# Second transform step as eight 64x32 matmul tiles side by side, its inverse as eight 32x64 tiles, complex products over all 128 partitions

## The chip, the cores and the metric

One Trainium2 chip (trn2), one core. The metric is the device time of one execution in microseconds, the median of several runs; lower is better.

Words used below: TensorE leaves its results in PSUM (the tiles `ps` and `pst` of the traces); an evacuation is the copy from there by ScalarE or VectorE (1.02 us for one of 128x1024 on ScalarE), after which the buffer is free again. A gemm is one of branch B's large matrix products. A burst is a row of branch A's matmuls between two pieces of gemm. A drain is the time that TensorE loses on entering and leaving a burst (0.22 us, measured in experiment 2). The granted clock is the share of TensorE's full clock that it was allowed in a stretch of the profile (1.0 or 0.5 in the profiled runs before and after).

## The reference

A forward and backward pass of two branches that share a layer norm. Branch A is a long convolution per channel by FFT (2048 points, 1024 channels) behind a four-tap shift filter; branch B is a gated MLP (1024 to 3584 and back). Cut to what matters:

```python
def _A_ref(q, k, v, shift_k, ssm_k, ssm_D):
    # kv = (k filtered by 4 taps) * v
    kv_f = rfft(pad(kv, 2S));  kf_f = rfft(pad(ssm_k, 2S))
    y = irfft(kv_f * kf_f)[:S] + kv * ssm_D
    return q * y
def _B_ref(x, W_gate, W_up, W_down):
    gate = x @ W_gate; up = x @ W_up
    return ((gate * (gate > 0)) * up) @ W_down
xn = layernorm(A_q)
out = A_q + _A_ref(xn, ...) + _B_ref(xn, ...)
# returned: out and the gradients of all nine inputs for grad_out
```

Per channel group of 128 (eight groups) the kernel needs three forward transforms (filter h, gradient g, product kv) and three inverse ones (gradient of kv, y, gradient of h). Each transform is two steps of small matmuls, with a transpose between them.

## The kernel before

TensorE runs the gemms of branch B all the time. The steps of branch A are a generator whose matmuls are put between the gemms', a few at each `yield`; `ns` is how much gemm time is to pass. Matmuls and loads get the current priority, ScalarE's and VectorE's work of the branch a late one, and a scheduler then orders every engine's queue at build time.

```python
def mm(self, out, lhsT, rhs, start=True, stop=True):
    self.pri.now();  self.nc.tensor.matmul(out, lhsT=lhsT, rhs=rhs, start=start, stop=stop)
def act(self, out, in_):           # nearly every evacuation of the branch's PSUM tiles: ScalarE (the transposes of h: VectorE, vcopy)
    self.pri.late(); self.nc.scalar.copy(out=out, in_=in_)
# self.ps: 2 PSUM buffers of 4 KB per partition for the whole branch; the gemms have 4 of 2 KB

def h_tile(self, st):              # filter: 32 transposes of 64 columns a group
    ...
    for r in range(16):
        for u in range(2):
            self.nc.tensor.transpose(pst[64*u:64*u+64, r, :], hv[:, r, u, :], self.identA[:])
    self.vcopy(hT[:, 0:16, :], pst[:])

def fwd2(self, Bf, F, ns):         # second step: 32 matmuls, 128x128 by 128 columns
    for k0 in range(0, NB1, 8):
        ps = self.ps.tile([P, 8, P], F32, name="ps2", tag="aps")
        for j in range(8):
            self.mm(ps[:, j, :], self.FW[:, k0 + j].rearrange("p a k -> p (a k)"), Bf[:, k0 + j, :])
        kh, kl = k0 // 16, k0 % 16
        rows = slice(64 * kh, 64 * kh + 64)
        self.act(F[rows, 0, kl:kl + 8, :], ps[0:64])      # real rows
        self.act(F[rows, 1, kl:kl + 8, :], ps[64:128])    # imaginary rows
        yield ns

def cmul(self, X, Z, conj, name):  # per half: products in full width, sums in 4 half-width ones
        ...
        self.tt(t1[:], X[:, :, ks, :], Z[:, :, ks, :], ALU.mult)
        self.tt(t2[:, 0], X[:, 0, ks, :], Z[:, 1, ks, :], ALU.mult)
        self.tt(t2[:, 1], X[:, 1, ks, :], Z[:, 0, ks, :], ALU.mult)
        for kh in range(2):
            rows = slice(64 * kh, 64 * kh + 64); kk = ...
            self.tt(Q[0:64, kk, :], t1[rows, 0], t1[rows, 1], ALU.add if conj else ALU.subtract)
            self.tt(Q[64:128, kk, :], t2[rows, 0], t2[rows, 1], ALU.subtract if conj else ALU.add)

def inv_a(self, Q, ns):            # inverse of the second step: 32 matmuls, 128x128 by 128 columns
    for k0 in range(0, NB1, 8):
        ps = self.ps.tile([P, 8, P], F32, name="ps3", tag="aps")
        for j in range(8):
            self.mm(ps[:, j, :], self.IA[:, k0 + j]..., Q[:, k0 + j, :])
        self.act(C[:, :, k0:k0 + 8, :], ps[:].rearrange("p k (cp i) -> p cp k i", i=2))
        ...
        yield ns
```

## Time and profile before

| | before |
|---|---|
| median of all runs of the first comparison | 1979.49 us (1974.76 to 1981.42) |
| TensorE busy in the profiled run | 1926.1 of 1974.6 us |
| VectorE, ScalarE busy | 988.9 us, 717.0 us |
| second step and its inverse: matmuls | 2 x 768, full array |
| first start to first start of the next gemm, 8 of these | 0.446 us |

How to read it: a matmul's duration in the profile is its latency (219 ns in the second step, where the next one starts after 0.056 us). What it costs TensorE's stream is the distance from its start to the next one's, so bursts are read from the start of the first matmul to the start of the gemm's next one. The lines themselves stand in the prediction.

### The profile page before, as it was taken

How to read it: one execution, taken by the hardware profiler on the slowest of the kernel's cores; microseconds unless marked ns; L12 is line 12 of the kernel's file. 1: busy time of each engine (PE TensorE's matmuls, PEld its weight loads, DVE VectorE, ACT ScalarE, POOL GpSimd, SP SyncE). 2: the span in 40 equal slices, each digit the busy share in tenths (PEclk: the TensorE clock that was granted, in tenths of full speed). 3: DMA queues.
4: the chain of work that ended last, by engine and by line, in shares of the span. 5: the costliest groups of instructions: out<-in, count | busy, mean ns of one | idle time of the engine just before them, and what ended most of it. 6: DMA issues, size and time to landing. Idle time of an engine off the chain costs nothing.

```text
span 1974.6 us, 27321 instructions
## 1 busy us (share of the span) xinstructions
PE 1926.1 (98%) x11022; PEld 916.2 (46%) x11022; DVE 988.9 (50%) x1457; ACT 717.0 (36%) x945; POOL 15.5 (1%) x36
## 2 busy tenths in 40 slices
PE   6899999999999999999999999999999999999998
PEld 3345445445444444444444445544444444444443
DVE  5879669578677756556356437300122122222222
ACT  5675365456446428347346455411000000000000
POOL 1000000000000000000000000000000000000000
PEclk9999999999999999999999999999999999999999
DMA  9954666974675674372753442593999854455451
GB/s 264 254 156 134 173 184 162 213 196 128 168 189 127 196 205 139 97 197 75 216 162 118 115 144 75 150 302 133 205 232 256 173 134 119 120 125 124 122 125 40
DMA packets 615168, 318.32 MB, mean 161 GB/s; under 512 B 450169, under 2 KB 584321, under 8 KB 615041
## 3 DMA queue, kind: packets, MB, share of 16 engines
q1 hardware_dynamic: 604544, 295.60, 58.7%
q10 hardware_dynamic: 9216, 16.78, 2.9%
q0 software_dynamic: 1280, 4.20, 0.6%
q8 instruction: 86, 1.41, 0.3%
q14 instruction: 42, 0.34, 0.1%
HBM read 141.36 MB, written 95.44 MB: 120 GB/s over the span
## 4 chain that ended last, share of the span: by engine, by line
PE 71%; DVE 4%; issue 2%; ACT 2%; DMA 1%; SPq 0%; DVEq 0%; ACTq 0%
PE ps_w L733 19%; PE ps_x L850 19%; PE ps_o L816 10%; PE ps_d L733 9%; PE ps L65 5%; PE ps_g L602 3%; PE ps_u L602 3%; PE ps_h L602 3%; ACT H L69 1%; DVE flp L291 1%; DVE t L73 1%; DVE ru L681 1%; PE pst L280 0%; DVE Y L73 0%; DVE ru L665 0%
## 5 line engine op out<-in xcount | busy, mean ns | idle before, releaser
L733 PE MATMUL ps_w<-ugs,xn_nat 128*128 128x512 bf16 x1792 | 402.6, 379 | 1.6 <-DMA xn_nat<-xn_d 1.6
L602 PEld LDWEIGHTS <-xnT 128*128 128x128 bf16 x1792 | 170.9, 98 | 212.0 <-issue 19.1
L733 PEld LDWEIGHTS <-xn_nat 128*128 128x128 bf16 x1792 | 170.2, 98 | 200.8 <-issue 7.2
L863 ACT ACTIVATE w<-xn,m 128x512 f32<-128x512 bf16 x32 | 24.3, 806 | 559.5 <-issue 317.2
L602 PE MATMUL ps_g<-wg,xnT 128*128 128x512 bf16 x896 | 210.4, 383 | 10.8 <-DVE ru L665 4.1
L602 PE MATMUL ps_h<-wdT,goT 128*128 128x512 bf16 x896 | 208.9, 381 | 3.0 <-DMA wdT<-in_B_W_down_dram 3.0
L733 PE MATMUL ps_d<-g_nat,hs 128*128 128x512 bf16 x896 | 204.8, 379 | 4.1 <-DMA hs<-h_d 4.1
L602 PE MATMUL ps_u<-wu,xnT 128*128 128x512 bf16 x896 | 206.4, 379 | 0.0
L850 PE MATMUL ps_x<-wuT,guT 128*128 128x512 bf16 x896 | 198.6, 379 | 0.0
L850 PE MATMUL ps_x<-wgT,ggT 128*128 128x512 bf16 x896 | 198.6, 379 | 0.0
L816 PE MATMUL ps_o<-wd,hT 128*128 128x512 bf16 x896 | 193.6, 379 | 0.0
L771 ACT CAST wi<-ps_w 128x512 bf16<-128x512 f32 x112 | 65.5, 586 | 207.2 <-PE ps_w L733 191.9
L680 ACT CAST gh<-ps_h 128x512 bf16<-128x512 f32 x112 | 65.4, 585 | 197.6 <-PE ps_h L602 126.0
L850 PEld LDWEIGHTS <-guT 128*128 128x128 bf16 x896 | 87.7, 98 | 105.7
L850 PEld LDWEIGHTS <-ggT 128*128 128x128 bf16 x896 | 87.7, 98 | 105.7
L816 PEld LDWEIGHTS <-hT 128*128 128x128 bf16 x896 | 87.7, 98 | 105.7
L602 PEld LDWEIGHTS <-goT 128*128 128x128 bf16 x896 | 85.2, 98 | 102.7 <-issue 10.1
L291 DVE STREAM_TRANSPOSE flp<-B 128x1024 f32<-128x1024 f32 x48 | 90.4, 1935 | 84.7 <-ACT B L69 84.5
L852 DVE CUSTOM_DVE_ANT_0 gx<-ps_x,gy 128x512 f32<-128x512 f32 x32 | 22.1, 692 | 217.9 <-PE ps_x L850 217.9
L733 PEld LDWEIGHTS <-hs 128*128 128x128 bf16 x896 | 83.8, 98 | 101.4 <-issue 5.9
L69 ACT CAST C<-ps 128x1024 bf16<-128x1024 f32 x96 | 97.3, 1017 | 61.1 <-PE ps L65 61.1
L291 DVE STREAM_TRANSPOSE flp<-C 128x1024 f32<-128x1024 f32 x48 | 89.8, 1928 | 52.6 <-ACT C L69 52.3
(156 smaller groups left out, 1699.7 us busy)
## 6 DMA issues: line engine op xcount, KB each, us to landing
ug_d<-ru SPq DMA_DIRECT2D x112, 256.0 KB, 3.0
ugs<-ug_d SPq DMA_DIRECT2D x112, 256.0 KB, 4.5
wg<-in_B_W_gate_dram SPq DMA_DIRECT2D x56, 256.0 KB, 4.2
wu<-in_B_W_up_dram SPq DMA_DIRECT2D x56, 256.0 KB, 3.9
h_d<-ht SPq DMA_DIRECT2D x112, 128.0 KB, 2.1
hs<-h_d SPq DMA_DIRECT2D x56, 256.0 KB, 4.3
out_dram<-wi SPq DMA_DIRECT2D x56, 256.0 KB, 2.5
gt<-in_grad_out_dram SPq DMA_DIRECT2D x32, 256.0 KB, 3.5
```

The lines of the kernel that those rows point to most:

```text
L65: self.nc.tensor.matmul(out, lhsT=lhsT, rhs=rhs, start=start, stop=stop)
L69: self.nc.scalar.copy(out=out, in_=in_)
L73: self.nc.vector.tensor_tensor(out=out, in0=in0, in1=in1, op=op)
L291: self.nc.vector.transpose(out=df[:, c0:c0 + 32, :], in_=sf[:, c0:c0 + 32, :])
L602: self.nc.tensor.matmul(ps[:], lhsT=xT[:, kt * P:(kt + 1) * P], rhs=w(kt), start=(kt == 0), stop=(kt == self.DT - 1))
L680: nc.scalar.copy(out=gh[:], in_=ps[:])
L733: self.nc.tensor.matmul(ps[:], lhsT=lhsT(st), rhs=rhs(st), start=(st == 0), stop=(st == self.ST - 1))
L771: nc.scalar.copy(out=wo[:, d, :], in_=ps[:])
L816: nc.tensor.matmul(ps[:], lhsT=hT[:, kt, :], rhs=self.wd[:, kt, oc], start=(kt == 0), stop=(kt == self.FT - 1))
L850: nc.tensor.matmul(ps[:], lhsT=T[:, kt, :], rhs=W[:, kt, oc], start=(i == 0), stop=(i == n - 1))
L852: V.tensor_tensor_reduce(out=gx[:, oc], in0=ps[:], in1=gy[:, oc], scale=1.0, scalar=0.0, op0=ALU.add, op1=ALU.add, accum_out=m[:, ob:ob + 1])
L863: nc.scalar.activation(out=w[:, oc], in_=xn[:, oc], func=ACT.Identity, scale=m[:, 5:6], bias=m[:, 4:5])
```

## The change

The intent: use the array for matmuls that fill it only in part by running eight at once, and get the spectra into a layout in which real and imaginary parts lie on the same partitions, so that the evacuation and the complex products work on all 128 partitions. The filter's first step becomes a full-array one for that layout. Core of the diff (tables and index arithmetic cut):

```diff
-        self.FW = con.tile([P, NB1, 2, 64], BF16, name="FW")
-        self.IA = con.tile([P, NB1, 2, 2, NB1], BF16, name="IA")
+        self.FW = con.tile([P, NB1, 2, NB1], BF16, name="FW")
+        self.IA = con.tile([P, 16, 2, 2, NB1], BF16, name="IA")
+        self.RH = con.tile([P, 2, 2, 2, NB1], BF16, name="RH")
 ...
     def h_tile(self, st):
         for r in range(16):
-            for u in range(2):
-                self.nc.tensor.transpose(pst[64 * u:64 * u + 64, r, :], hv[:, r, u, :], self.identA[:])
+            self.nc.tensor.transpose(pst[:, r, :], hv[:, r, :], self.identA[:])
 ...
+    def fwd1_filter(self, hT, sD, ns):          # h: full-array matmuls of 512 columns, 2 per yield
+                self.mm(ps[:, 512 * jj:512 * jj + 512], self.RH[:, r0 // 16]..., hT[:, r:r + 4, :]...)
 ...
     def fwd2(self, Bf, F, ns):
+        for j0 in range(0, 4, 2):
+            for j in range(j0, j0 + 2):
+                ps = self.ps.tile([P, 2, 2, 2, P], F32, name="ps2", tag="aps")
+                for ri in range(2):
+                    for m in range(2):
+                        for q in range(4):
+                            for e in range(2):
+                                rows, l = slice(64 * e, 64 * e + 64), 8 * q + 2 * j + m
+                                self.mm(ps[32 * q:32 * q + 32, e, ri, m, :], self.FW[rows, l, ri, :], Bf[rows, l, :])
+                self.act(F[:, 2 * j:2 * j + 2]..., ps[:]...)          # all 128 partitions
+            yield 2 * ns
 ...
     def cmul(...):
-            for kh in range(2): ... four sums over 64 partitions
+            self.tt(Q[:, g, 0], t1[:, :, 0], t1[:, :, 1], ALU.add if conj else ALU.subtract)
+            self.tt(Q[:, g, 1], t2[:, 0], t2[:, 1], ALU.subtract if conj else ALU.add)
 ...
     def inv_a(self, Q, ns):
+        for j0 in range(0, 4, 2):
+            ps = [self.ps.tile([P, 2, 2, 2, P], F32, name="ps3", tag="aps") for _ in range(2)]
+            for j in range(2):
+                for m in range(2):
+                    for ri in range(2):
+                        for q in range(4):
+                            for e in range(2):
+                                rows, x = slice(32 * q, 32 * q + 32), 8 * e + 2 * (j0 + j) + m
+                                self.mm(ps[q // 2][64 * e:64 * e + 64, q % 2, j, m, :], self.IA[rows, x, ri]...,
+                                        Q[rows, 2 * (j0 + j) + e, ri, P * m:P * m + P], start=ri == 0, stop=ri == 1)
+            for h in range(2):
+                self.act(C[:, :, 2 * h:2 * h + 2, 2 * j0:2 * j0 + 4, :], ps[h][:]...)
+            yield 2 * ns
```

## The prediction

> **What bounds the kernel now.** I read the page first (busy times, slices, the chain), then the groups by shape, the TensorE waits, and three short stretches of the TensorE timeline, because the change lives inside a few bursts of matmuls.
>
> The page (busy line; TensorE and ScalarE in 40 slices; the chain):
> ```profile
> PE 1926.1 (98%) x11022; PEld 916.2 (46%) x11022; DVE 988.9 (50%) x1457; ACT 717.0 (36%) x945; POOL 15.5 (1%) x36
> ...
> PE   6899999999999999999999999999999999999998
> ...
> ACT  5675365456446428347346455411000000000000
> ...
> PE 71%; DVE 4%; issue 2%; ACT 2%; DMA 1%; SPq 0%; DVEq 0%; ACTq 0%
> ```
> See: TensorE is at nine tenths or more in every slice but the first two and the last. The transform branch (slices 3 to 26, where ScalarE is busy) never makes it fall below that. So the time is what TensorE streams, plus small pauses; VectorE and ScalarE work counts only where TensorE waits for it.
>
> TensorE's own waits between 98 and 1290 us, where the branch runs:
> ```profile
> PE ps L65 <- ACT H L69: 5.1, 9, 1.4
> PE ps_g L602 <- DVE ru L665: 4.1, 3, 2.2
> PE ps_d L733 <- DMA hs<-h_d: 4.1, 3, 1.8
> PE ps L65 <- DVE flp L291: 2.0, 2, 1.1
> ```
> See: what ScalarE and VectorE cost TensorE is about 11 us in total (the first, second and fourth lines), so even a large saving there can bring no more than this.
>
> The groups the change touches, by shape:
> ```profile
> L69 ACT CAST H<-ps 64x1024 bf16<-64x1024 f32 x64 | 64.4, 1006 | 6.9 <-PE ps L65 5.7
> L65 PE MATMUL ps<-flp,FW 128*128 128x128 bf16 x768 | 58.5, 219 | 1.3 <-DVE flp L291 1.0 <-ACT H L69 0.4
> ...
> L73 DVE TENSOR_TENSOR GH<-t 64x1024 bf16<-64x1024 bf16 x64 | 43.8, 684 | 0.9
> ...
> L280 PE MATMUL pst<-ident,hn 128*64 128x128 bf16 x256 | 16.0, 278 | 0.0
> L280 PEld LDWEIGHTS <-hn 128*64 128x64 bf16 x256 | 14.9, 204 | 3.0 <-issue 3.0
> ```
> The 219 ns of a matmul is its latency; what it takes from the stream is the distance to the next start. The timeline gives that (start, length, what, count):
> ```profile
> 115.46 1.89 PE L602 MATMUL ps_h<-wdT,goT 128*128 128x512 bf16 x8
> 117.18 0.61 PE L65 MATMUL ps<-flp,FW 128*128 128x128 bf16 x8
> 117.63 1.89 PE L602 MATMUL ps_h<-wdT,goT 128*128 128x512 bf16 x8
> ...
> 195.73 3.62 PE L602 MATMUL ps_u<-wu,xnT 128*128 128x512 bf16 x16
> 199.28 1.05 PE L65 MATMUL ps<-flp,RB 128*64 128x512 bf16 x8
> 200.26 3.63 PE L602 MATMUL ps_h<-wdT,goT 128*128 128x512 bf16 x16
> ...
> 218.12 1.08 PE L65 MATMUL ps<-kp,gks 128*32 128x128 bf16 x64
> 219.13 1.04 PE L602 MATMUL ps_g<-wg,xnT 128*128 128x512 bf16 x4
> ```
> See three things. The eight second-step matmuls take 117.63 - 117.18 = 0.45 us, 0.056 us each, and the eight gemm matmuls before them 1.72 us, 0.216 each: no pause on entering or leaving. The 64 column-tiled matmuls of the tap gradient take 219.13 - 218.12 = 1.01 us, 0.0158 each: four tiles really do run side by side (0.056/4 = 0.014), with some 0.1 us left over. And the burst in two column tiles: from 195.73 to 200.26 is 4.53 us, of which 16 x 0.216 = 3.46 and four side-by-side rounds x 0.216 = 0.86 are stream; 0.21 us remain. A burst in another tile shape therefore costs about 0.2 us to enter and leave.
>
> [...] The transposes of h now have 64 columns and their loads show 204 ns against 98 for a contiguous 128x128; whether a strided load of 128 columns is faster, no row shows. [...]
>
> **The change, part by part.** The second step and its inverse are each called 24 times (8 groups, 3 spectra).
>
> Second step and inverse, TensorE. Before: 2 x 768 full-array matmuls x 0.056 = 86 us, in the gemm's own shape, so no drains. After: 128 small matmuls per call, eight side by side, so 16 rounds instead of 32 matmuls: 2 x 24 x 16 x 0.056 = 43 us if eight tiles run as four do. But each burst now leaves the gemm's shape. The order of the built kernel has 49 bursts for the second step (47 of 64 matmuls, 2 of 32) and 55 for the inverse (46 of 64, the rest fragments): 104 x 0.2 = 21 us. So 86 becomes 64: -22 us. Half the stream is saved and half of that is given back to drains.
>
> First step of the filter: before 64 matmuls 64x512 in pairs, 32 rounds x 0.216 = 6.9, plus 17 bursts x 0.2 = 3.4; after 64 full-array ones x 0.216 = 13.8 without drains: +3.5 us.
>
> Transposes of h: before 256 of 64 columns. The first 32 start at 93.68 and the gemm follows at 95.60, so 1.92 us per group, 8 x 1.92 = 15.4. After: 128 of 128 columns, no drain. At 0.056 each (load hidden) 7.2 us; at 0.11, the pace of the present pairs, 14.1; at 0.22, if a strided column costs what it costs now and nothing is loaded in parallel, 28. I choose 0.09, 11.5 us: -4 us.
>
> ScalarE: 192 copies of 64x1024 at 1006 ns become 96 of 128x1024 at about 1020 (the B and C rows' sort): 193 to 98 us, -95 us. The other copies keep their number. VectorE: the four half-width sums per half product become two in full width; 192 rows of 684 ns become 96 of the 128x1024 form, 685 ns, so 131 to 66 us, -66 us. Neither is on the path, except for the 11 us of waits. I give half of these back: -6 us, with one shortened cold-clock spell after the 2.2 us wait counted in. Table building shrinks by a few us of ScalarE and VectorE work early on, beside TensorE: 0.
>
> Sum: -22 + 3.5 - 4 - 6 = -28.5, which from 1977.6 gives 1949. I put the prediction at 1952, for the rival that follows.
>
> **The rivals.** (a) Eight tiles don't get fed. A burst is 128 instructions in 8 x 0.056 = 0.45 us, 3.5 ns each; in the tap gradient the same 128 take 1.01 us, so nothing in this trace shows such a pace. [...] Within the tap burst pairs start about 4 ns apart[...], which speaks for it. If decoding only holds the tap gradient's pace, 6144 x 0.014 = 86 us plus 21 us of drains stand against 86: +21, and the total is about 1993. In between ([...]0.64 us a burst) the gain of 22 nearly vanishes: about 1970.
> (b) The evacuation paces it. The inverse takes both PSUM buffers of the branch in one burst, and the second step fills both too, so the next burst waits for two ScalarE copies, 2.04 us, plus one or two of the gemm's of 0.59. Between bursts lie about 16 gemm matmuls, 3.46 us. That just fits; where it doesn't, TensorE pauses. At 0.1 us per burst this is +10 us: about 1960.
> (c) The relief is worth more than its waits, since VectorE's complex products stand before the gemm's own VectorE step (the 2.2 us wait on ru). All 11 us and some drains less: about 1940.
> (d) The strided loads of h come out at 0.22 us: +13 in place of -4, about 1968.
>
> **Range and chances.** The full-rate case (six in ten) lies at 1940 to 1958, the partial one (three in ten) at 1958 to 1978, the unfed one (one in ten) above. Low 1937, high 1975. 2% is 39.5 us, so faster needs under 1938: the 29 us plus 11 from elsewhere. Faster 0.11, within 2% 0.85, slower 0.04.
>
> **What would show it.** Right: the second step's 64 small matmuls take about 0.45 us to the next gemm start minus the drain (0.55 us with it), the inverse the same; the gap before them is about 0.1 us over 0.216; TensorE's waits on H and ru fall; TensorE busy stays at 97 to 98%; ScalarE falls to about 620 us and VectorE to about 920. Wrong: bursts of 0.7 us and more[...], waits of the branch's matmuls on ScalarE's C, F or K copies growing, transposes of h at 0.2 us each. The prediction falls if the burst is longer than 0.7 us, or if the time drops by more than 40 us, which would mean that the branch's VectorE and ScalarE work held TensorE in a way its waits don't show.

In rival (a) the 0.64 us a burst was an assumed value, and "decoding" stands for whatever sets the pace of the tap gradient's burst (0.0158 us a matmul measured). The "cold-clock spell" is in the trace: 3.4 us at a granted clock of 0.5 after the wait of 2.24 us that ends at 498.90.

## More of the kernel before

After branch A has ended, `out_phase` begins; ScalarE's queue issues its loads `ya`, `xe`, `xr` into a pool that is laid into the memory which branch A's pools had. The tables `FW` and `IA` took 8 KB per partition each.

## The result, and the profile after

The changed kernel takes 1968.46 us (1965.94 to 1969.93, 4 runs) against 1979.49 before. The ratio is 0.9946, 95% interval 0.9924 to 0.9969. Ratios here are the mean time of one kernel's runs over that of the other's of the same rounds, so not quite the ratio of the medians that are quoted. The step is clear of noise, but it is 11 us where 25 to 28 were foretold.

The page of the changed kernel, the same lines as shown of before:
```profile
PE 1894.5 (96%) x15264; PEld 881.7 (45%) x15502; DVE 912.3 (46%) x1374; ACT 615.8 (31%) x852; POOL 15.3 (1%) x37
...
PE   6899999999999989999999999899999999999998
...
ACT  5654354344444425444344444311000000000000
...
PE 87%; DMA 4%; DVE 4%; issue 3%; ACT 1%; SPq 0%; ACTq 0%; DVEq 0%
```
ScalarE lost 101 us and VectorE 77, about as foretold (to 622 and 923). TensorE stays the bound. Of its matmul records 238 are missing (15264 of 15502; the weight loads are complete), so its busy time and the "0.16 <-issue" remarks below are partly gaps in the record; where the gemm's first matmul after a burst is missing, its weight load dates it.

The groups by shape (columns: busy us, mean ns, idle before):
```profile
L66 PE MATMUL ps<-flp,FW 64*32 64x128 bf16 x3072 | 36.2, 221 | 1.6 <-DVE flp L302 1.0 <-ACT B L70 0.5
...
L70 ACT CAST H<-ps 128x1024 bf16<-128x1024 f32 x32 | 30.9, 1019 | 10.8 <-PE ps L66 10.8
...
L74 DVE TENSOR_TENSOR GH<-t 128x1024 bf16<-128x1024 bf16 x32 | 20.8, 685 | 0.0
...
L291 PEld LDWEIGHTS <-hn 128*128 128x128 bf16 x128 | 9.3, 150 | 1.4
```
A full-width copy or sum takes what a half-width one took (1019 against 1006 ns, 685 against 684), so their number is what counts. The strided load of 128 columns takes 150 ns where the one of 64 took 204 (a contiguous 128x128 takes 98); step and tile shape differ at once between the two, so no run parts them. 16 transposes follow each other at 0.063 us.

The first bursts of the second step on TensorE's timeline:
```profile
117.96 1.89 PE L636 MATMUL ps_h<-wdT,goT 128*128 128x512 bf16 x8
119.78 0.75 PE L66 MATMUL ps<-flp,FW 64*32 64x128 bf16 x64
...
125.75 0.75 PE L66 MATMUL ps<-flp,FW 64*32 64x128 bf16 x64
126.43 0.82 PE L636 MATMUL ps_u<-wu,xnT 128*128 128x512 bf16 x2
```
In the second burst shown no record is missing: 126.43 - 125.75 = 0.68 us from the first small matmul to the gemm. Before it the gap is 119.78 - 117.96 - 8 x 0.216 = 0.09 us. So a burst of 64 costs 0.78 us, not the 0.65 of the prediction's sum (0.45 and 0.2).

The start times of single records show where in the burst it goes. These are read from the same trace (ns from the burst's first start; number of the matmul in the burst):

```
matmul   1   2   8 |   9  16 |  17  24 |  25  32 |  33   34   35   36  ...  63   64
start    0   4  24 |  66  90 | 122 145 | 178 201 | 253  261  270  278  ... 503  537
```

Four rounds of eight come every 56 ns, as hoped: eight tiles do run side by side. Then, after exactly 32 matmuls and 33 weight loads (the 33rd load starts at 181 ns), 65 instructions, there is a pause of 52 ns, and from there on a matmul every 8.3 ns, with its load in between: 4.17 ns per instruction in the mean. Of the 93 whole bursts of both kinds 92 show the break at this place.

A second thing is new at the end of branch A. TensorE and, under it, ScalarE and VectorE in the same stretch:
```profile
1252.79 0.76 PE L66 MATMUL ps<-GH,IA 32*64 32x128 bf16 x64
1253.71 13.11 PE L767 MATMUL ps_w<-ugs,xn_nat 128*128 128x512 bf16 x59 [0.16 <-issue]
1273.38 1.89 PE L66 MATMUL ps<-RB,flp 128*128 128x64 bf16 x32 [6.56 <-DVE flp L302]
```
```profile
1253.56 1.01 ACT L70 CAST C<-ps 128x1024 bf16<-128x1024 f32 x1 [1.80 <-PE ps L66]
1253.69 0.34 ACTq L835 DMA_DIRECT2D ya<-y_d  x1
...
1263.11 0.59 ACT L805 CAST wi<-ps_w 128x512 bf16<-128x512 f32 x1 [7.11 <-DMA xe<-xn_d]
...
1268.65 1.02 ACT L70 CAST C<-ps 128x1024 bf16<-128x1024 f32 x1
```
```profile
1269.69 3.63 DVE L302 STREAM_TRANSPOSE flp<-C 128x1024 f32<-128x1024 f32 x2 [1.94 <-ACT C L70]
```
The last inverse ends on TensorE at 1253.6. One of its two C copies runs at once; the other is in ScalarE's queue behind the loads ya, xe and xr of the next phase, which wait for buffers and for each other (the last is issued at 1267.79), and starts at 1268.65. The flip follows, and TensorE, which has run out of gemms put before this point, waits 6.56 us. Before the change ScalarE's queue held those loads behind the last C copy.

From the start times of all matmuls I take, for each part, the time from the end of the gemm before it (last start and 0.216) to the start of the gemm after it. Sums in us of the two profiled runs:

| part | foretold | before | after | change |
|---|---|---|---|---|
| second step, 95 and 49 bursts | } -22 | 44.8 | 39.1 | -5.8 |
| its inverse, 99 and 55 bursts | } | 45.7 | 40.7 | -5.0 |
| transposes of h | -4 | 16.0 | 8.1 | -7.9 |
| first step of h | +3.5 | 11.2 | 19.0 | +7.8 (4.9 of it two waits on the copy of h) |
| first step of kv | (waits: -6) | 17.0 | 10.1 | -6.9 (its waits on ScalarE gone) |
| last step of h's inverse | 0 | 8.7 | 16.3 | +7.7 (the wait above) |
| pauses inside the gemms | (in the -6) | 23.4 | 25.9 | +2.5 |

They add to -7.6, where the two profiled runs differ by 7.5.

A third thing the sums hide. The first of the two waits on the copy of h ends at 406.06 us, and after it TensorE is granted half its clock for 3.4 us (`--windows`: length, busy time of each engine, granted clock, DMA):
```profile
406.20:409.60 3.40, 3.18 (x8) 1.18 (x8) 1.68 (x5) 1.01 (x1) 0.00 (x0) 0.50 0.46 116
```
The weight loads of the gemm there, which are all on record, come every 0.43 us and not every 0.216, so this wait of 2.8 us cost some 1.7 us more. Between 98 and 1290 us the kernel before has one such stretch (3.4 us at 499, after a wait of 2.24 us), the changed kernel three (3.4 us at 406, 3.4 at 710, 6.8 from 1270 on, the last one beginning within the wait of 6.56 us): 13.6 us for 3.4, which can have cost 5.1 us at most (half of the 10.2 us more).

### The profile page after: what moved, and what is told of

Its sections match the earlier page's. It is cut to its first block, busy times and chain, and to the rows that moved or that the text cites. A ratio compares the mean times of both kernels' runs of the same rounds, so it can differ in the third digit from the quotient of the medians.

```text
span 1967.1 us, 35885 instructions
## 1 busy us (share of the span) xinstructions
PE 1894.5 (96%) x15264; PEld 881.7 (45%) x15502; DVE 912.3 (46%) x1374; ACT 615.8 (31%) x852; POOL 15.3 (1%) x37
## 4 chain that ended last, share of the span: by engine, by line
PE 87%; DMA 4%; DVE 4%; issue 3%; ACT 1%; SPq 0%; ACTq 0%; DVEq 0%
PE ps_w L767 19%; PE ps_x L884 19%; PE ps_o L850 10%; PE ps_d L767 10%; PE ps_h L636 8%; PE ps_u L636 8%; PE ps_g L636 8%; PE ps L66 6%; DMA h_d<-ht 1%; DVE flp L302 1%; DVE ru L699 1%; DMA ln_x<-in_A_q_dram 0%; DVE tap L74 0%; DMA g_nat<-in_grad_out_dram 0%; DMA xe<-xn_d 0%
## 5 line engine op out<-in xcount | busy, mean ns | idle before, releaser
L767 PE MATMUL ps_w<-ugs,xn_nat 128*128 128x512 bf16 x1731 | 391.6, 380 | 8.1 <-issue 4.5
L767 PE MATMUL ps_d<-g_nat,hs 128*128 128x512 bf16 x863 | 197.9, 381 | 8.0 <-DMA g_nat<-in_grad_out_dram 3.9
L636 PE MATMUL ps_u<-wu,xnT 128*128 128x512 bf16 x866 | 201.6, 379 | 2.8 <-issue 1.9
L70 ACT CAST C<-ps 128x1024 bf16<-128x1024 f32 x96 | 92.6, 1016 | 53.0 <-PE ps L66 51.9
```

The lines of the kernel that those rows point to most:

```text
L636: self.nc.tensor.matmul(ps[:], lhsT=xT[:, kt * P:(kt + 1) * P], rhs=w(kt), start=(kt == 0), stop=(kt == self.DT - 1))
L767: self.nc.tensor.matmul(ps[:], lhsT=lhsT(st), rhs=rhs(st), start=(st == 0), stop=(st == self.ST - 1))
```

## The experiments

All were run on a chip beside the kernel before; the ratio is to it. `e1_pad` is an edit of the changed kernel; all later ones are edits of `e1_pad`, except `e10_before_h_early`, which is one of the kernel before. All gave correct results but one.

**1. The buffers back where they lay.** `e1_pad`:
```diff
         self.gs_all = con.tile([P, self.NG, 4], F32, name="gs_all")
+        self.pad = con.tile([P, 3840], BF16, name="pad")
+        V.memset(self.pad[:, 0:2], 0.0)
```

> The changed kernel with one unused 7.5 KB tile added beside the tables, so that the branch's other buffers lie where they lay before the change; no arithmetic differs. Theory (the smaller tables moved the next phase's buffers, its loads were put ahead of the last inverse copy on ScalarE, and TensorE stood 6.6 us for the last flip): that wait goes, the last two bursts of 16 are apart again, and the time is 6 to 8 us under the changed kernel's, about 1961, 0.990 to 0.992 of before. Rival (the wait has another cause, or the loads are only late by chance): the time stays within 2 us of the changed kernel's, 0.994 to 0.995 of before. The small bursts cost 0.78 us each in both.

Measured: 1963.14 us, ratio 0.9920 (0.9907 to 0.9932), so some 5 us under the changed kernel's 0.9946, a little less than expected; the two intervals, of different rounds, still overlap, and the profiled spans differ by 6.7. The same stretch on TensorE and on ScalarE:
```profile
1254.28 0.76 PE L66 MATMUL ps<-GH,IA 32*64 32x128 bf16 x64
...
1263.62 0.63 PE L66 MATMUL ps<-RB,flp 128*128 128x64 bf16 x16
```
```profile
1255.05 1.93 ACT L70 CAST C<-ps 128x1024 bf16<-128x1024 f32 x2 [1.80 <-PE ps L66]
...
1268.25 0.41 ACTq L837 DMA_DIRECT2D ya<-y_d  x1
```
Both C copies run at once, the loads follow 11 us later, and the wait is gone, by nothing but an unused tile. The stall is an effect of where the smaller tables let the next phase's buffers lie.

**2. Bursts of 32.** `e2_bursts32`:
```diff
                 self.act(F[:, 2 * j:2 * j + 2]..., ps[:]...)
-            yield 2 * ns
+                yield ns
 ...  in inv_a, inside the loop over j:
+                if j == 0:
+                    yield ns
 ...
-            yield 2 * ns
+            yield ns
```

> As e1_pad, but each burst of 64 small matmuls is cut into two of 32 with gemm matmuls between (some 96 more bursts). Theory ([...]32 pairs, run at eight tiles side by side, 0.0070 us each; only what comes after them is held to 0.0083 after a pause of 0.05): a burst of 32 takes 4 x 0.056 + 0.19 = 0.41 us, none shows the pause, and the total is 96 x (2 x 0.41 - 0.78) = 4 us above e1_pad, in a range of 2 to 8. Rival (eight tiles are slow throughout[...]): a burst of 32 streams at 0.0090 each, takes 0.48 us, and the total is 96 x 0.19 = 18 us above e1_pad.

Measured: 1974.97 us, ratio 0.9981 (0.9967 to 0.9994): 12 us above `e1_pad`, between the two expectations. The bursts decide it:
```profile
116.96 1.89 PE L640 MATMUL ps_h<-wdT,goT 128*128 128x512 bf16 x8
118.78 0.42 PE L66 MATMUL ps<-flp,FW 64*32 64x128 bf16 x32
119.35 1.67 PE L640 MATMUL ps_h<-wdT,goT 128*128 128x512 bf16 x7 [0.16 <-issue]
```
The gemm's first record is missing; its weight load dates it to 119.13. Over all bursts of 32 the median, with the gap before, is 0.442 us for the second step (0.455 for the inverse), and none of the second step's 92 has the break after its 32nd matmul, for there is none. Four rounds of 0.056 are 0.223, so entering and leaving costs 0.219, a little more than the 0.19 I had put in. The rival, slow tiles throughout, wanted 0.48. Two of 0.442 against one of 0.776 for 46 pairs is +5.0 us, two of 0.455 against 0.786 for 47 pairs +5.8, together 10.8; my 4 had the drains too small. That this is close to the 12 is partly luck. In the sums over all bursts the inverse takes 11.2 us more than in `e1_pad`, since 21 of its bursts stand 0.27 to 0.41 us in their middle (in the one at 193.48 us ScalarE is still copying C until 193.81), and the pauses inside the gemms are 6.0 us less: the wait on g_nat near 700 us, 4.0 us in `e1_pad`, isn't there. The medians leave both out. They also give the price of the break: at the full rate a burst of 64 would take 0.445 + 0.219 = 0.66 and takes 0.78, so 0.11 to 0.12 us, some 11 us over 93 bursts.

**3. What holds the second half.** `e5_n64`, wrong:
```diff
-    self.mm(ps[32 * q:32 * q + 32, e, ri, m, :], self.FW[rows, l, ri, :], Bf[rows, l, :])
+    self.mm(ps[32 * q:32 * q + 32, e, ri, m, 0:64], self.FW[rows, l, ri, :], Bf[rows, l, 0:64])
```

> Wrong results on purpose: as e1_pad, but the second step's small matmuls stream 64 columns instead of 128 (the same values are copied out twice). It measures what holds the second half of a burst to 0.0083 us per pair. If it is the rate at which instructions are handed on (a fixed time per instruction), the second half stays at 0.0083 and a burst still takes at least 0.55 us with its 0.22 of entering and leaving. If it is the eight tiles' streaming or conflicts between them, it falls towards half. [...]

Measured in one look (1959.84 us, results wrong as intended). A burst:
```profile
119.72 0.70 PE L66 MATMUL ps<-flp,FW 64*32 64x64 bf16 x64
120.35 1.90 PE L640 MATMUL ps_h<-wdT,goT 128*128 128x512 bf16 x8
```
120.35 - 119.72 = 0.63 where 128 columns took 0.68. Its start times: the first 32 matmuls begin within 124 ns, in rounds of 29 ns where 128 columns took 56; the next one begins at 227 ns, and from there a matmul every 8.3 ns again. So half the columns halve the rounds of the first half and leave the second's pace alone: that pace is the same time per pair with both widths, 4.17 ns per instruction in the mean. The weight loads, the same in both kernels, can start faster than that: the first 33 of this burst come 3.3 ns apart. The pause is not a fixed time: it is 103 ns here for 52 with 128 columns, and in both kernels the first matmul after it starts 27 to 28 ns after the first small matmul of the burst has ended by its record (226 ns long with 128 columns, 199 with 64; new starts at 253 and 227). By the records 65 instructions have started when the pause begins. What holds the next ones back until then is not shown. The pace falls in with the first branch of my expectation.

**4. The relief given back.** `e3_half_width`:
```diff
-                self.act(F[:, 2 * j:2 * j + 2]..., ps[:]...)
+                for rows in (slice(0, 64), slice(64, 128)):
+                    self.act(F[rows, 2 * j:2 * j + 2]..., ps[rows]...)
 ...
-            self.tt(Q[:, g, 0], t1[:, :, 0], t1[:, :, 1], ...)
-            self.tt(Q[:, g, 1], t2[:, 0], t2[:, 1], ...)
+            for rows in (slice(0, 64), slice(64, 128)):
+                self.tt(Q[rows, g, 0], t1[rows, :, 0], t1[rows, :, 1], ...)
+                self.tt(Q[rows, g, 1], t2[rows, 0], t2[rows, 1], ...)
```

> As e1_pad, but the second step's ScalarE copies and the sums of the complex products are done in two halves of 64 partitions, which gives back the 95 us of ScalarE and the 66 us of VectorE that the change saved; TensorE's instructions are the same. Theory (TensorE sets the time, the relief counts only in its waits): 2 to 9 us above e1_pad. Rival (the relief is what the change earned, the small tiles earn nothing): 15 us or more above e1_pad, that is no better than before.

Measured: 1981.16 us, ratio 1.0015 (1.0000 to 1.0029). The rival was right: 18 us above `e1_pad`, no better than before, with TensorE's bursts still at 0.776. TensorE's waits here (total, times, longest):
```profile
PE ps_g L640 <- DVE ru L703: 5.0, 5, 1.5
...
PE ps L66 <- ACT H L70: 3.7, 7, 1.1
...
PE ps L66 <- ACT C L70: 3.6, 2, 2.9
```
Summed over all bursts, second step, inverse and first step of kv take 5.9 + 4.1 + 4.0 = 14 us more than in `e1_pad`, and the pauses inside the gemms 9 us more, with the 5.0 of the first line; the first step of h takes 2 us less. These waits are not those of before given back; they are larger than them. My theory fell here.

**5. Which half of it.** `e8_act_half` has the first edit of the last experiment alone, `e9_dve_half` the second.

> As e1_pad, with the second step's ScalarE copies alone in two halves (95 us of ScalarE given back). If the 18 us of e3_half_width come from the evacuation, which a burst that fills both PSUM buffers cannot run ahead of: 10 to 15 us above e1_pad, and e9_dve_half within 4 us. If they come from VectorE's complex products standing before the gemm's own VectorE steps: within 4 us of e1_pad here, 10 to 15 above there. If they add: both in between.

> As e1_pad, with the sums of the complex products alone in two halves (66 us of VectorE given back). Numbers as told for e8_act_half: within 4 us of e1_pad if evacuation is the cause of the 18 us, 10 to 15 above it if VectorE's queue is.

Measured: 1975.56 us, ratio 0.9981 (0.9968 to 0.9994), with ScalarE's 95 us given back, and 1970.06 us, ratio 0.9961 (0.9948 to 0.9974), with VectorE's 66. That is 12 and 8 us above `e1_pad`'s 0.9920, and together about the 18 of both. They add, though by the recorded numbers the first alone lies in its branch of 10 to 15; per 10 us of added work each costs TensorE 1.2 to 1.3 us. In `e8_act_half` TensorE's waits show where: ScalarE's copies, mostly. In `e9_dve_half` 4.8 us more are pauses inside the gemms, among them 2.1 us of waits on ru, and 4.1 us lie in the inverse, 3.3 of them in one burst at 334 us.
```profile
PE ps L66 <- ACT H L70: 3.7, 7, 1.1
PE ps L66 <- ACT C L70: 3.1, 2, 2.4
...
PE ps L66 <- ACT G L70: 1.9, 2, 1.3
```

**6. The filter's path as before.** `e6_filter_back`: the transposes of 64 columns and the 64-row first step, as before the change (short form of the edit):
```diff
-        yield from self.fwd1_filter(hT, st["sD"], 2000)
+        yield from self.fwd1(hT, 2000, add_D=st["sD"])   # and h_tile as before
```

> As e1_pad, but the filter h is transposed in 64 columns and goes through the first step in 64-row pairs, as before the change. From the trace of the changed kernel this part cost 25.6 us of TensorE (8.1 transposes, 17.5 first step with 4 us of waits) against 27.2 before it: so 1 to 3 us above e1_pad, not to be told from it. If the full-width transposes or the waits on them matter more than the account says: 6 us or more, in either direction.

Measured: 1963.32 us, ratio 0.9922 (0.9910 to 0.9935), not to be told from `e1_pad`. Its transposes and first step take 16.0 + 11.9 us, those of `e1_pad` 8.1 + 19.6, so 28 us in both: the account by start times holds. (The 25.6 us in the expectation counted this part 1.5 us too low.) This part of the change neither gained nor lost.

**7. More room before the first step of h.** `e7_h_early`:
```diff
             hT = self.h_tile(st)
-            yield 2000
+            yield 5000
 ...
             self.store(self.out_gh[cg, :], ghf)
-            yield 6000
+            yield 3000
```

> As e1_pad, with 3 us more of gemm between the transposes of h and the first step that needs them (and 3 us less at the end of each group). The trace of e1_pad shows TensorE waiting 3.1 and 1.9 us on the copy of h. Theory: these waits go, 3 to 5 us under e1_pad, 0.989 to 0.990 of before. Rival (other waits take their place, the sum of the branch's VectorE work being what it is): within 2 us of e1_pad, 0.991 to 0.993.

Measured: 1950.38 us, ratio 0.9859 (0.9844 to 0.9873): 12 us under `e1_pad`, more than twice the expected. TensorE's waits in the branch's stretch:
```profile
PE ps_w L769 <- DMA xn_nat<-xn_d: 2.9, 4, 1.3
PE ps_d L769 <- DMA g_nat<-in_grad_out_dram: 1.2, 1, 1.2
PE ps L66 <- DVE hT L78: 1.2, 1, 1.2
```
By start times 4.0 us come from the first step of h, 2.9 from the inverse of Y (the scheduler had torn two of its bursts into nine pieces, each with its own drains; now one is in three), 1.4 from the second step and 1.3 from the last step of h's inverse. The pauses inside the gemms are 2.0 us less; about 1 us of that lies in the layer norm, before the edit acts (the first transposes of h start at 95.34 us and not at 96.46), and I don't know why. What the expectation left out is the clock: `e1_pad` runs 3.4 us at half clock after the wait on the copy of h at 406 us and 6.8 us from 707 on, `e7_h_early` only 3.4 us at 699, which can have given up to 3.4 of the 12 us. The mean granted clock of all its runs is higher too, 0.9965 against 0.9942.

**8. The same move in the kernel before, and the move taken further.** `e10_before_h_early` makes the edit of `e7_h_early` in the kernel before; `e11_h_earlier` moves all 6 us (8000 and 0).

> The kernel before, with the same move of 3 us of gemm ahead of the filter's first step as e7_h_early, to see whether that gain belongs to the change. If the waits that e7_h_early removed are those of the changed kernel (the copy of h, the torn bursts of the inverse of Y): within 4 us of before, 0.998 to 1.002. If the old placing cost both alike: 9 to 12 us under before, 0.994 to 0.995, and the change is worth only what e1_pad shows (0.992).

> As e7_h_early, with the other 3 us moved as well (8 us of gemm between the transposes and the first step, none at the end of a group). One wait of 1.4 us on the copy of h is left in the trace of e7_h_early. Theory: 0 to 3 us under it, 0.984 to 0.986 of before, as what is left lies in the phase changes. Rival (the last inverse's copies now run into the next group's): 3 us or more above it.

Measured: 1977.03 us, ratio 0.9983 (0.9960 to 1.0006), and 1961.07 us, ratio 0.9903 (0.9888 to 0.9918). The kernel before gains nothing that can be told from noise (its six runs lie 14 us apart), so the gain, as far as the runs tell, belongs to the changed one. Moved further, it is lost again: 9 us above `e7_h_early`. The order of its build has a burst of the inverse of GKV torn into pieces of 7 to 27 instead, its waits name the flip with 3.5 us and the copies of yt and gks with 2.4, and 10.2 us run at half clock again, as in `e1_pad`. The placing wants measuring; I have no rule for it.

## Why the prediction was right or wrong

- TensorE as the bound, and eight tiles at 0.056 us per round: right. ScalarE's and VectorE's savings, 101 and 77 us: right.
- Second step and inverse, -22: wrong by half; it came to -10.8. The step that failed is "16 rounds ... if eight tiles run as four do", with 0.45 us per burst of 64; it measured 0.56 (0.78 less 0.22 of drains). `e2_bursts32` and `e5_n64` show that this holds for the first 32 matmuls with their loads, 65 instructions with the 33rd load, and that the rest come at 4.17 ns per instruction after a pause: 0.11 to 0.12 us per burst, 11 us. It was named as the first rival, with an assumed 0.64 us a burst and about 1970 in its partial case, and given three chances in ten. What the runs show is the break after the 32nd matmul, in 92 of 93 bursts, and the pace of 8.3 ns per pair after it. The drains were close: 0.22 measured for 0.2. The 0.0158 us that the prediction reads for a matmul of the tap gradient is a mean over the burst, drain included, and not the distance of two tiles' starts; within a round that is 3.4 ns here. That the total fell so near the 1970 of the partial case is in part luck, since the stall of the next point is in it; without it `e1_pad` gives 1963.
- The 7.7 us at the end of the branch: not in the prediction at all. No step asked what the smaller tables do to the addresses of later pools, and the built order, which I had counted bursts in, already showed the loads ahead of the last copy.
- "Even a large saving there can bring no more than this" (11 us): the number of the waits before was taken as a bound on what ScalarE's and VectorE's relief is worth. `e3_half_width` shows 18 us for the changed kernel. The reason I take for it, argued and not tested alone: a burst that fills both PSUM buffers depends more on its evacuation than one that fills one of them. This would be the mechanism of the second rival, seen from the other side: the wide copies keep it small, and small tiles with half-width copies and sums earn nothing (that part `e3_half_width` shows). In the total the step did no harm: first step of kv -6.9 against -6 for all waits.
- Filter, +3.5 and -4: the sum was right (-0.5 foretold, -0.1 measured, no difference in `e6_filter_back`), the terms were not, which is luck; the transposes came to 0.063 us each, for 0.09, and two waits on the copy of h took the gain.
- The pauses inside the gemms rose by 2.5 us in the profiled runs. The layer norm alone ends 2.9 us later (first transposes of h at 96.62 us for 93.68). In the branch's stretch the waits on ru (4.1 us) are gone, but TensorE ran 13.6 us at half clock for 3.4. The prediction counted on the one stretch that it saw being shortened; it is gone, and no step asked for new ones after new waits. No experiment was made on these pauses alone; this stays open.

The forecast of 1952 is thus missed by 16 us: 11 for the bursts and 7.7 for the stall, with smaller errors of both signs beside them.

## What to carry to other kernels

Small matmuls side by side were paid here in instructions (8.3 ns per pair after the 32nd, for 7.0 in the rounds before) and drains (0.22 us a burst): measure both, and ask whether the next burst's buffers are free, before multiplying rounds. The waits that a profile shows bound a relief only as long as the structure of the work stays (11 us of waits before, 18 us lost in `e3_half_width`); that a kernel which fills its buffers in larger lumps needs the relief that the old one could do without is my reading, not tested alone. Count a wait of some us together with the clock after it: here 2.8 us of waiting were followed by 3.4 us at half clock, for another 1.7. And after a change in the size of any buffer, look at the build's order for later phases that have moved forward in a queue: an unused tile was worth 5 us, and 3 us of gemm in another place 12.
